# Three edits to a four-batch attention and feed-forward kernel: narrower column tiles for one batch's value products, two weights taken by halves of the tokens, one load placed three steps on

## The chip, the cores and the metric

The kernel runs on one core of a Trainium2 chip. The metric is the device time of one execution in microseconds. Before the change it is 664.37 us, the median of three runs (662.48, 664.87 and 664.37).

## What is computed

Four batches of 768 tokens and eight heads of 64 go through a local attention with block summaries, then through a token-mixing product and a two-layer feed-forward part. Cut to what matters:

```
B, H, S, D = 4, 8, 768, 64                  block, window = 32, 16
k_sum = max over each block of 32 keys      v_sum = mean over each block of 32 values
scores = concat(q k^T / 8 where |i-j| < 16, q k_sum^T / 8 + log 32)
a = softmax(scores)                          x = a @ concat(v, v_sum)      (heads side by side: 768 x 512)
u = x + (x^T U V)^T                          U: 768 x 32, V: 32 x 768
out = u + max(u @ w_ch1, 0) @ w_ch2          w_ch1: 512 x 2048, w_ch2: 2048 x 512
```

## The kernel before

**Staging.** Batch 0's attention runs alone at the start, in an order written out by hand in the string `START`; each word is one step of one head and half (`S` scores, `E` exponentials, `T` transposes, `C` their copies, `V` value products, `N` normalising, `M` block means and so on). Then the feed-forward part of batch 0 runs with the attention of batch 1 between its products, and so on: while TensorE works through batch b's feed-forward part (`up_phase`, 54 steps, then `down_phase`, 96 steps, one for each of 16 weight blocks times 6 tiles of 128 tokens), the attention of batch b+1 is dealt out between these steps.

**Value products of batch 0.** `values(st, h, a)` (L471 to L486) multiplies, for each of three tiles of 128 queries, the exponentials of 64 queries (the stationary operand, 120 rows by 64 columns) with the 120 value rows that this half sees (65 columns wide, the last of ones). The two halves of a tile go to the two halves of the output's partitions, so each instruction uses half of the array's columns. A float32 matmul of the program is two MATMUL records in the trace, so that the 96 matmuls of batch 0 are 192 records at L480. The later batches do the same with `square_values` (L488), by 32 queries and with a tile position for each quarter (L494). `block_means` (L293) also works by 32 columns, alternating between two of the four quarters in one call; `spread_v` (L1016) and `mix_t` (L667) work by 32 columns too.

**The later batches' attention.** `later_step(st, i)` (L544) is step i of 32 for batches 2 and 3. Every third step starts a head. The first 15 steps are spread over the 54 steps of the up phase at places `4 + i * 50 // 15`, so step 2 stands at place 10, step 5 at 20, step 8 at 30, step 7 at 27 and step 10 at 37. The value summaries of heads 4 to 7 need the block sums of the values: `load_vsum(st, 1, i)` (L239) issues two DMAs of 128 x 512 float32 (256 KB each, L253) into buffers of the tag `val`, of which there are eight and which the outputs `o` use too; `add_vsum` (L256) queues the halving adds of these two on GpSimd, one for each step of the phase (`drip`). The sums are first read by step 16, which stands in the down phase, as a copy by ScalarE (L340).

**Queues.** All DMAs are issued by SyncE in program order, those of the weights (`fetch_weight`, L874 to L879, names `whole`) among them. ScalarE casts each fetched weight (L186), takes the exponentials (L413), copies the value summaries (L340) and copies the products of the up phase out of PSUM (L1236, L1248, L1261, L1224), all in program order. TensorE's next product into a bank waits for such a copy.

**The end.** In `down_phase` the six accumulators `acc` stand in six banks; weight block f goes over the six token tiles, three matmuls each (high and low parts). After block 15's three matmuls of a tile, VectorE adds its accumulator to `x` (L1295). Then, for the last batch, `finish` (L1300) runs eight times, for two halves of the tokens and four blocks of 128 columns: three transposes into a bank `ps_o` (L740), a copy by ScalarE (L1303), and a DMA of 192 KB (L1305). `gates` (L1268) prepares the next block's operands `gh` and `gl` on ScalarE and VectorE (L1271, L1272); both have two buffers.

Of the kernel before, what the change touches and what calls it, by code (L numbers as in the profile page):

```python
# [31 lines left out]
DV = D + 1  # L32
NC = DM // P
NF = DF // P
# [52 lines left out]
def body(ctx: ExitStack, tc, q0, q1, k, v, vn, uv, w1, w2, mask, ident, rep, out):  # L87
    nc = tc.nc
# [10 lines left out]
    def bank(name):  # L99
        return psum.tile([P, 512], F32, name=name, tag="bank")  # L100
# [33 lines left out]
    for i in range(4):  # L134
        t = op_place(i)
# [81 lines left out]
    def load_qk(st, h):  # L217
        load_k(st, h)
        load_q(st, h)
# [19 lines left out]
    def load_vsum(st, g, i):  # L239

        parts = 2
        n = BLOCK * D // (2 * parts)
        spare = None
        if st.b == 1 or st.b == 2 and g == 0:
            spare = hidden_place(2 + i)
        st.vn[g, i] = []
        for j in range(parts):
            if spare is not None:
                t = spare[:, j * n : (j + 1) * n]
            else:  # L250
                t = mo.tile([P, DM], F32, name="stage", tag="val", bufs=VALS)[:, :n]
            k = i * parts + j
            nc.sync.dma_start(out=t, in_=vn[st.b, g, :, k * n : (k + 1) * n])  # L253
            st.vn[g, i].append(t)

    def add_vsum(st, g, i):  # L256

        for j, t in enumerate(st.vn.pop((g, i))):
            n = t.shape[1] // 2
            while n > D:  # L260
                nc.gpsimd.tensor_tensor(t[:, :n], t[:, :n], t[:, n : 2 * n], ALU.add)
                yield
                n //= 2
            if i == 0 and j == 0:
                st.vsum[g] = small.tile([P, DV], F32, name="vsum")
                nc.gpsimd.memset(st.vsum[g][:, D:], 1.0)
                nc.gpsimd.tensor_tensor(st.vsum[g][:, :D], t[:, :D], t[:, D : 2 * D], ALU.add)
                yield
            else:
                nc.gpsimd.tensor_tensor(t[:, :D], t[:, :D], t[:, D : 2 * D], ALU.add)  # L270
                yield
                nc.gpsimd.tensor_tensor(st.vsum[g][:, :D], st.vsum[g][:, :D], t[:, :D], ALU.add)
                yield
        if i == 1:
            nc.gpsimd.tensor_scalar_mul(st.vsum[g][:, :D], st.vsum[g][:, :D], 1.0 / BLOCK)
# [193 lines left out]
        copy(at.rearrange("k i q -> k (i q)"), ps[:KC, : 3 * P])  # L469

    def values(st, h, a):  # L471
        at = st.at.pop((h, a))
        if h not in st.psx:
            st.psx[h] = bank("ps_x")
        ps = st.psx[h]
        vt = st.vt[h]
        for i in range(3):
            u = 3 * a + i
            for t in range(2):
                nc.tensor.matmul(  # L480
                    ps[64 * t : 64 * t + 64, u * DV : (u + 1) * DV],
                    at[:, i, 64 * t : 64 * t + 64],
                    vt[u % 2][:, (u // 2) * 2 + (t + u) % 2],
                    start=True,
                    stop=True,
                )  # L486

    def square_values(st, h):  # L488
# [44 lines left out]
    slow = []  # L533
# [10 lines left out]
    def later_step(st, i):  # L544

        h, a = divmod(i, 3)
        if a == 0:  # L550
            if 1 <= h <= H:
                send_squares(st, h - 1)
            if 2 <= h <= H + 1:
                fetch_squares(st, h - 2)
            if h < H:
                scores_by_subtiles(st, h)
                exponentials(st, h, 0)
            if 3 <= h <= H:
                load_v(st, h - 1)
        elif a == 1:  # L560
            if h < H:
                exponentials(st, h, 1)
            if h + 1 < H:
                key_maxima(st, h + 1)
            if 1 <= h <= H:
                for t in range(2):
                    value_summaries(st, h - 1, t, nc.scalar.copy)
        else:
            if h + 2 < H:
                load_qk(st, h + 2)  # L570
            if h == 2:
                st.x = mo.tile([P, NU, DM], F32, name="x")
            if 2 <= h <= H + 1:
                square_values(st, h - 2)
                normalise(st, h - 2)
            if h < H:
                turn_squares(st, h)
        if i in (2, 5):
            load_vsum(st, 1, i // 5)
        if i in (4, 7):  # L580
            slow.append(add_vsum(st, 1, i // 7))
        if i in MIX:
            mix(st, 2 * MIX.index(i))
        if i - 1 in MIX:
            mix_back(st, 2 * MIX.index(i - 1))
# [323 lines left out]
    def use_weight(*key):  # L909
        want, t = prepared[len(used)]  # L910
        assert want == key
        used.append(key)
        return t if key[0] == "down" else [t[:, i] for i in range(t.shape[1])]
# [62 lines left out]
    st = sts[0]  # L976
# [114 lines left out]
    steps = one_bank_steps(nxt)  # L1091
# [70 lines left out]
    for f in range(NF):  # L1162
        for hf in range(2):
            g = first.pop() if first else up_out(up(st, hf, f))
# [103 lines left out]
    def gates(st, f):  # L1268
        h = st.h[f // 2][:, f % 2]
        gh, gl = gate_place("gh"), gate_place("gl")  # L1270
        nc.scalar.activation(gh, h, AF.Relu)  # L1271
        nc.vector.scalar_tensor_tensor(gl, h, 0.0, f32(gh), ALU.max, ALU.subtract)  # L1272
        return gh, gl

    def down_phase(st, g):

        acc = []
        for f in range(NF):
            w = use_weight("down", f)
            ahead = gates(st, f + 1) if f + 1 < NF else None  # L1280
            gh, gl = g
            for t in range(NU):
                if f == 0:
                    acc.append(bank(f"acc{t}"))
                sl = slice(t * P, (t + 1) * P)
                for j, (part_w, gt) in enumerate(((0, gh), (0, gl), (1, gh))):
                    nc.tensor.matmul(  # L1287
                        acc[t],
                        gt[:, sl],
                        w[:, part_w],  # L1290
                        start=(f == 0 and j == 0),
                        stop=(f == NF - 1 and j == 2),
                    )
                if f == NF - 1:
                    nc.vector.tensor_tensor(st.x[:, t], st.x[:, t], acc[t], ALU.add)  # L1295
                yield
            prepare()
            g = ahead

    def finish(st, hf, c):  # L1300
        ps = turn_tokens(st, hf, c)
        o = mo.tile([P, DM], F32, name="o", tag="val", bufs=8)[:, :NH]
        nc.scalar.copy(o, ps)  # L1303
        t0 = st.b * S + hf * NH
        nc.sync.dma_start(out=out[c, :, t0 : t0 + NH], in_=o)  # L1305

    def spread(items, first, last):

        at = {}
        for i, x in enumerate(items):  # L1310
            at.setdefault(first + i * (last - first) // len(items), []).append(x)
        return at

    UP, DOWN = 7 * NF // 2 - 2, NF * NU
# [8 lines left out]
    behind = [(finish_first, hf, c) for hf in range(2) for c in range(NC)]  # L1323
    for b in range(1, B):
        cur, ahead, after = ([*sts, None, None][b + i] for i in range(3))
        todo = later_steps(ahead) if ahead else []
        mine, theirs = todo[:FIRST_STEPS], todo[FIRST_STEPS:]
        steps = spread(mine, 4, UP)
        ends = spread(behind, 2, 2 + 2 * len(behind))
        phase = up_phase(cur)  # L1330
        for i in itertools.count():
            try:
                next(phase)
            except StopIteration as end:
                last = end.value
                break
            do(steps.get(i, ()))
            do(ends.get(i, ()))
            tick()
            drip()  # L1340
            if i == UP - 4:
                g = gates(cur, 0)
        steps = spread(theirs, 0, DOWN - 5)
        for i, x in enumerate(last):
            steps.setdefault(1 + 2 * i, []).insert(0, x)
        for i, _ in enumerate(down_phase(cur, g)):
            do(steps.get(i, ()))
            tick()
            drip()
            if after and i % NU == 0:  # L1350
                do([(later_start, after, j) for j in {10: (-6,), 11: (-5,), 12: (-4,), 13: (-3, -1), 14: (-2,)}.get(i // NU, ())])
        behind = [(finish, cur, hf, c) for hf in range(2) for c in range(NC)]
    do(behind)


# [91 lines left out]
```

## Time and profile before

| | |
|---|---|
| median of three runs | 664.37 us |
| the profiled execution: own time, span | 663.06 us, 661.3 us |
| TensorE busy in the span | 638.6 us (97%), 5232 matmul records |
| VectorE, ScalarE, GpSimd busy | 374.4, 357.5, 361.5 us |
| granted TensorE clock over the span | 0.999 |
| moved by DMA | 115.24 MB by one queue, 57.7% of 16 engines' span |
| read from HBM, written | 91.10 MB, 24.12 MB |

The page of the profile gives each engine's busy time, the span in 40 slices, the DMA queues, the chain of work that ended last, the costliest groups of instructions and the DMA issues. The trace gives the instructions in order of time, merged where they are alike, with the idle time of the engine before them and what ended it in brackets; PE is TensorE, PEld its weight loads, DVE VectorE, ACT ScalarE, POOL GpSimd, SPq the queue of SyncE. A table of windows gives each engine's busy time in stretches of the span.

### The profile page before, as it was taken

Reading aid. Unit: us, or ns where it says so; the run is one execution under the profiler, and the core shown is the slowest. Engines: PE = TensorE matmul, PEld = TensorE weight load, DVE = VectorE, ACT = ScalarE, POOL = GpSimd, SP = SyncE. Lnnn points to the kernel's source line nnn. Section 1 sums busy time; section 2 is a strip of 40 time slices with the busy share of each in tenths; the row PEclk is TensorE's granted clock in tenths of the full one; section 3 lists DMA queues with packets and bytes.
Section 4 is the critical chain, followed back from the end, with each engine's and each line's share of the span. In section 5 each row is a group of like instructions: output and inputs, shape, how many; then the busy total and the mean of one; then the engine's idle time right before and its main releaser. Section 6 shows DMA issues by size and latency. Waiting matters only on the chain.

```text
span 661.3 us, 14015 instructions
## 1 busy us (share of the span) xinstructions
PE 638.6 (97%) x5232; PEld 561.1 (85%) x5232; DVE 374.4 (57%) x1008; ACT 357.5 (54%) x801; POOL 361.5 (55%) x402
## 2 busy tenths in 40 slices
PE   5899999999999998999999999999999999999996
PEld 5789888989888998987887899997787899998885
DVE  5578777658678586576544645566554522232223
ACT  4666666654663547665553467665453465553322
POOL 5423985966586777751355577761344365653310
PEclk9999999999999999999999999999999999999999
DMA  8997497765874169796455069786441055342002
GB/s 215 227 371 229 146 303 237 229 205 183 237 227 158 55 218 314 205 263 195 141 147 161 25 194 339 227 249 193 146 121 57 24 184 168 112 127 65 32 1 95
DMA packets 76420, 116.13 MB, mean 176 GB/s; under 512 B 6976, under 2 KB 52928, under 8 KB 76352
## 3 DMA queue, kind: packets, MB, share of 16 engines
q1 hardware_dynamic: 76352, 115.24, 57.7%
q8 instruction: 41, 0.67, 0.4%
q14 instruction: 27, 0.22, 0.1%
HBM read 91.10 MB, written 24.12 MB: 174 GB/s over the span
## 4 chain that ended last, share of the span: by engine, by line
PE 83%; DMA 5%; DVE 4%; ACT 3%; POOL 2%; issue 1%; SPq 1%; ACTq 0%; POOLq 0%; DVEq 0%
PE acc L1287 30%; PE ps_h L1202 24%; PE acc L943 8%; PE ps_h L921 7%; PE ps_x L494 3%; PE ps_s L354 3%; PE ps_o L740 2%; PE ps_s L377 2%; DMA place<-in_q 1%; DMA qz<-in_q 1%; PE ps_m L667 1%; DMA whole<-up 1%; PE ps_t L463 1%; PE ps_x L480 1%; POOL parts L187 1%
## 5 line engine op out<-in xcount | busy, mean ns | idle before, releaser
L187 POOL TENSOR_TENSOR parts<-whole,parts 128x512 fp32r<-128x512 f32 (+1 forms) x144 | 181.7, 1271 | 154.2 <-ACT parts L186 144.7
L1287 PE MATMUL acc<-parts,gh 128*128 128x512 f32 x576 | 192.3, 399 | 0.0
L1202 PE MATMUL ps_h<-op,parts 128*128 128x384 f32 x1008 | 186.5, 338 | 2.2 <-ACT place L1261 1.8
L1202 PEld LDWEIGHTS ps_h<-op,parts 128*128 128x128 f32 x1008 | 173.8, 188 | 5.1 <-ACT place L1261 2.1
L1287 PEld LDWEIGHTS acc<-parts,gh 128*128 128x128 f32 x576 | 108.1, 188 | 23.7 <-issue 1.7
L1287 PE MATMUL acc<-parts,gl 128*128 128x512 f32 x288 | 112.6, 391 | 0.0
L1272 DVE SCALAR_TENSOR_TENSOR gl<-place,gh 128x768 fp32r<-128x768 f32 x48 | 56.2, 1171 | 97.1 <-ACT gh L1271 97.1
L186 ACT CAST parts<-whole 128x512 fp32r<-128x512 f32 (+1 forms) x144 | 83.6, 584 | 8.2 <-DMA whole<-up 7.1
L921 PE MATMUL ps_h<-place 128*128 128x384 f32 x384 | 74.5, 342 | 0.0
L1271 ACT ACTIVATE gh<-place 128x768 fp32r<-128x768 f32 x48 | 40.6, 846 | 60.0 <-PE acc L1287 59.9
L413 ACT ACTIVATE e<-e,neg 128x120 f32<-128x120 f32 x144 | 46.3, 386 | 48.5 <-DVE neg L403 46.0
L943 PE MATMUL acc<-place,gh 128*128 128x512 f32 x192 | 68.4, 410 | 1.3 <-POOL place L187 1.3
L921 PEld LDWEIGHTS ps_h<-place 128*128 128x128 f32 x384 | 65.8, 188 | 1.0 <-DVE place L722 0.3
L162 POOL TENSOR_SCALAR val<-place 128x512 f32<-128x512 f32 (+1 forms) x30 | 47.0, 1583 | 30.7 <-ACT place L149 14.3
L1287 PEld LDWEIGHTS acc<-parts,gl 128*128 128x128 f32 x288 | 54.2, 188 | 9.9 <-DVE gl L1272 0.3
L187 POOL TENSOR_TENSOR place<-val,place 128x512 fp32r<-128x512 f32 x29 | 39.3, 1377 | 18.6 <-ACT place L186 18.6
L187 POOL TENSOR_TENSOR op<-tmp,op 128x384 fp32r<-128x384 f32 x24 | 25.4, 1069 | 39.2 <-ACT op L186 39.2
L943 PEld LDWEIGHTS acc<-place,gh 128*128 128x128 f32 x192 | 35.6, 188 | 10.5 <-POOL place L187 3.2
L403 DVE CUSTOM_DVE_ANT_0 e<-ps_s,mask_sb 128x120 f32<-128x120 f32 x144 | 32.4, 276 | 12.1 <-PE ps_s L377 7.3
L943 PE MATMUL acc<-place,gl 128*128 128x512 f32 x96 | 37.6, 392 | 0.0
L933 ACT ACTIVATE gh<-ps_h 128x384 fp32r<-128x384 f32 x32 | 15.7, 492 | 36.3 <-PE ps_h L921 36.0
L1262 DVE TENSOR_TENSOR place<-place,ps_h 128x384 f32<-128x384 f32 x24 | 13.3, 554 | 33.6 <-ACT place L1261 33.6
(124 smaller groups left out, 861.2 us busy)
## 6 DMA issues: line engine op xcount, KB each, us to landing
place<-in_w SPq DMA_DIRECT2D x32, 512.0 KB, 5.8
whole<-up SPq DMA_DIRECT2D x24, 512.0 KB, 3.9
whole<-down SPq DMA_DIRECT2D x24, 512.0 KB, 3.7
whole<-up SPq DMA_DIRECT2D x24, 384.0 KB, 3.5
vt<-in_v SPq DMA_DIRECT2D x48, 146.2 KB, 3.9
kt<-in_k SPq DMA_DIRECT2D x24, 288.0 KB, 5.1
out_t<-o SPq DMA_DIRECT2D x32, 192.0 KB, 2.4
there<-squares SPq DMA_DIRECT2D x16, 384.0 KB, 4.3
```

What stands on the lines that cost most here:

```text
L162: nc.gpsimd.tensor_scalar(f32(bits), f32(hi), 0.0, None, ALU.mult)
L186: nc.scalar.copy(hi, val)
L187: engine.tensor_tensor(lo, val, f32(hi), ALU.subtract)
L354: nc.tensor.matmul(ps[:, i * KC : (i + 1) * KC], qt[:, 64 + j * P : 64 + j * P + P], kt[:, k0 : k0 + KC], start=True, stop=True,)
L403: nc.vector.tensor_tensor_reduce(out=e[:, u, :], in0=ps[:, i * KC : (i + 1) * KC], in1=mask_sb[:, m, :], scale=-SCALE, scalar=BIG, op0=ALU ...
L413: nc.scalar.activation(e[:, u, :], e[:, u, :], AF.Exp, bias=st.neg[h][:, u : u + 1], scale=-1.0,)
L921: nc.tensor.matmul(ps[:, :NH], w_split[0, f][:, c % 2, part_w, c // 2], ut[:, c, :], start=(n == 0), stop=(n == 3 * NC - 1),)
L943: nc.tensor.matmul(acc[t], gt[:, sl], w_split[1, f][:, part_w], start=(first and j == 0), stop=(last and j == 2),)
L1202: nc.tensor.matmul(ps, a[:, sa, i], b[:, sb, i], start=(first and n == 0), stop=(n == 5), skip_group_check=not first,)
L1271: nc.scalar.activation(gh, h, AF.Relu)
L1272: nc.vector.scalar_tensor_tensor(gl, h, 0.0, f32(gh), ALU.max, ALU.subtract)
L1287: nc.tensor.matmul(acc[t], gt[:, sl], w[:, part_w], start=(f == 0 and j == 0), stop=(f == NF - 1 and j == 2),)
```

## The change

**Value products of batch 0 by 32 queries.** Each matmul of 64 stationary columns becomes two of 32, with a tile position, in the order of the four quarters; the moving operand and the outputs stay.

**Loads of the value sums three steps on.** For batches 2 and 3, the two `load_vsum` of heads 4 to 7 go from the ends of steps 2 and 5 to those of steps 5 and 8, and their adds from steps 4 and 7 to steps 7 and 10.

**The last two weight blocks by halves of the tokens.** For the last batch, the order of the last twelve steps of the down phase becomes block 14 tiles 0 to 2, block 15 tiles 0 to 2, block 14 tiles 3 to 5, block 15 tiles 3 to 5. The four `finish` of the first half of the tokens go behind steps 91, 92, 93 and 94 of 0 to 95, and only the four of the second half stay behind the phase; of these, the copies of the odd column blocks go to VectorE.

```
     def values(st, h, a):
...
-            for t in range(2):
+            for n in range(4):
                 nc.tensor.matmul(
-                    ps[64 * t : 64 * t + 64, u * DV : (u + 1) * DV],
-                    at[:, i, 64 * t : 64 * t + 64],
-                    vt[u % 2][:, (u // 2) * 2 + (t + u) % 2],
+                    ps[32 * n : 32 * n + 32, u * DV : (u + 1) * DV],
+                    at[:, i, 32 * n : 32 * n + 32],
+                    vt[u % 2][:, (u // 2) * 2 + (n // 2 + u) % 2],
                     start=True,
                     stop=True,
+                    tile_position=(0, 32 * n),
                 )
...
-        if i in (2, 5):
-            load_vsum(st, 1, i // 5)
-        if i in (4, 7):
-            slow.append(add_vsum(st, 1, i // 7))
+        if i in (5, 8):
+            load_vsum(st, 1, i // 8)
+        if i in (7, 10):
+            slow.append(add_vsum(st, 1, i // 10))
...
     def down_phase(st, g):
-        acc = []
-        for f in range(NF):
-            w = use_weight("down", f)
-            ahead = gates(st, f + 1) if f + 1 < NF else None
-            gh, gl = g
-            for t in range(NU):
...
+        order = [(f, t) for f in range(NF) for t in range(NU)]
+        if st.b == B - 1:
+            order[-2 * NU :] = sorted(order[-2 * NU :], key=lambda ft: (ft[1] >= NU // 2, ft))
+        acc, got = [], {}
+        for f, t in order:
+            if f not in got:
+                got[f] = (use_weight("down", f), *g)
+                g = gates(st, f + 1) if f + 1 < NF else None
+            w, gh, gl = got[f]
...
     def finish(st, hf, c):
...
-        nc.scalar.copy(o, ps)
+        (nc.vector.tensor_copy if (st.b, hf) == (B - 1, 1) and c % 2 else nc.scalar.copy)(o, ps)
...
         steps = spread(theirs, 0, DOWN - 5)
+        if b == B - 1:
+            for c in range(NC):
+                steps[DOWN - 5 + c] = [(finish, cur, 0, c)]
...
-        behind = [(finish, cur, hf, c) for hf in range(2) for c in range(NC)]
+        behind = [(finish, cur, hf, c) for hf in range(b == B - 1, 2) for c in range(NC)]
```

The first place is TensorE's order near the end of batch 0's attention; `ps_x` are the value products, `ps_v`, `ps_m` and `ps_r` small products of the mixing part. Before:

```order
L463 MATMUL ps_t<-ident_sb,gh 120x128 x6
L480 MATMUL ps_x<-place 64x65 x18
L1016 MATMUL ps_v<-place,ident_sb 32x192 x8
L480 MATMUL ps_x<-place 64x65 x6
L667 MATMUL ps_m<-x,u_sb 32x128 x6
L1016 MATMUL ps_v<-place,ident_sb 32x192 x8
L667 MATMUL ps_m<-x,u_sb 32x128 x6
L685 MATMUL ps_r<-t_766,rep_sb 128x128
L480 MATMUL ps_x<-place 64x65 x12
L667 MATMUL ps_m<-x,u_sb 32x128 x6
```

and the same place of the changed kernel, where the lines stand one or two further down:

```order
L463 MATMUL ps_t<-ident_sb,gh 120x128 x6
L481 MATMUL ps_x<-place 32x65 x36
L1018 MATMUL ps_v<-place,ident_sb 32x192 x8
L481 MATMUL ps_x<-place 32x65 x12
L669 MATMUL ps_m<-x,u_sb 32x128 x6
L1018 MATMUL ps_v<-place,ident_sb 32x192 x8
L669 MATMUL ps_m<-x,u_sb 32x128 x6
L687 MATMUL ps_r<-t_850,rep_sb 128x128
L481 MATMUL ps_x<-place 32x65 x24
L669 MATMUL ps_m<-x,u_sb 32x128 x6
```

The sequence stays; each group of value products has twice as many, of 32 columns, and stands beside other products of 32 columns.

The second place is SyncE's queue in the up phase of batch 1, while batch 2's attention is dealt out; `stage` are the value sums' loads, `whole` the weights' fetches, `o` the outputs of batch 0. Before:

```order
L208 DMA kt<-in_k 128x3x192
L214 DMA qz_84<-in_q 64x3x128
L215 DMA qz_84<-in_q 64x4x128
L253 DMA stage<-in_vn 128x512 x2
L969 DMA out_t<-o 128x384
L878 DMA whole<-up_109 128x768
L969 DMA out_t<-o 128x384
L438 DMA there<-squares 128x768
L969 DMA out_t<-o 128x384
L878 DMA whole<-up_110 128x1024
L969 DMA out_t<-o 128x384
L878 DMA whole<-up_110 128x768
```

and of the changed kernel, from the output that stood behind the loads:

```order
L971 DMA out_t<-o 128x384
L880 DMA whole<-up_109 128x768
L971 DMA out_t<-o 128x384
L438 DMA there<-squares 128x768
L971 DMA out_t<-o 128x384
L880 DMA whole<-up_110 128x1024
L971 DMA out_t<-o 128x384
L880 DMA whole<-up_110 128x768
L208 DMA kt<-in_k 128x3x192
L214 DMA qz_85<-in_q 64x3x128
L215 DMA qz_85<-in_q 64x4x128
L253 DMA stage<-in_vn 128x512 x2
```

The first two loads move behind three weight fetches, four outputs, one store of squares and the next head's keys and queries, to the place where the second two stood; the second two move to the same place one head later.

The third place is TensorE's order at the very end; `acc` are the accumulators of the six token tiles in order of their numbers, `ps_o` the transposes of `finish`. Before:

```order
L1287 MATMUL acc_7409<-parts,gh 128x512
L1287 MATMUL acc_7409<-parts,gl 128x512
L1287 MATMUL acc_7413<-parts,gh 128x512
L1287 MATMUL acc_7413<-parts,gl 128x512
L1287 MATMUL acc_7413<-parts,gh 128x512
L740 MATMUL ps_o<-ident_sb,x 128x128 x24
```

and of the changed kernel:

```order
L742 MATMUL ps_o<-ident_sb,x 128x128 x3
L1296 MATMUL acc_7505<-parts,gh 128x512
L1296 MATMUL acc_7505<-parts,gl 128x512
L1296 MATMUL acc_7505<-parts,gh 128x512
L742 MATMUL ps_o<-ident_sb,x 128x128 x3
L1296 MATMUL acc_7509<-parts,gh 128x512
L1296 MATMUL acc_7509<-parts,gl 128x512
L1296 MATMUL acc_7509<-parts,gh 128x512
L742 MATMUL ps_o<-ident_sb,x 128x128 x12
```

Half of the transposes move in front of the last matmuls, and the other half stays behind them.

More of the change, by code (lines that the diff above doesn't have):

```diff
@@ L1275, in down_phase @@
     def down_phase(st, g):
-        acc = []
-        for f in range(NF):
-            w = use_weight("down", f)
-            ahead = gates(st, f + 1) if f + 1 < NF else None
-            gh, gl = g
-            for t in range(NU):
[L1283 to L1298, printed above, removed]
+        order = [(f, t) for f in range(NF) for t in range(NU)]
[7 more added lines that the diff above has]
+            w, gh, gl = got[f]
+            if f == 0:
+                acc.append(bank(f"acc{t}"))
+            sl = slice(t * P, (t + 1) * P)
+            for j, (part_w, gt) in enumerate(((0, gh), (0, gl), (1, gh))):
+                nc.tensor.matmul(
+                    acc[t],
+                    gt[:, sl],
+                    w[:, part_w],
+                    start=(f == 0 and j == 0),
+                    stop=(f == NF - 1 and j == 2),
+                )
+            if f == NF - 1:
+                nc.vector.tensor_tensor(st.x[:, t], st.x[:, t], acc[t], ALU.add)
+            yield
+            if t == NU - 1:
+                prepare()
     def finish(st, hf, c):
```

## The prediction

> **What bounds the kernel now.** I read the page first, then the table of windows, to find the stretches in which TensorE (PE) idles, and there the instructions in order of time.
>
> ```profile
> span 661.3 us, 14015 instructions
> PE 638.6 (97%) x5232; PEld 561.1 (85%) x5232; DVE 374.4 (57%) x1008; ACT 357.5 (54%) x801; POOL 361.5 (55%) x402
> ```
>
> PE is busy for 638.6 of 661.3 us, and no other engine for over 57%. PE bounds the kernel, and an edit gains only where it shortens PE's work or one of its waits: 22.7 us in all, most of them at the two ends.
>
> ```profile
> core 0: us, PE busy (x) PEld busy (x) DVE busy (x) ACT busy (x) POOL busy (x), PEclk, DMA share, GB/s
> 240.00:250.00 10.00, 10.00 (x81) 9.48 (x79) 8.75 (x29) 4.25 (x11) 4.46 (x6) 1.00 0.92 291
> 250.00:260.00 10.00, 8.18 (x66) 7.53 (x65) 4.91 (x12) 7.30 (x19) 9.19 (x15) 1.00 1.02 318
> 260.00:270.00 10.00, 10.00 (x120) 9.25 (x119) 6.36 (x23) 6.29 (x15) 7.62 (x11) 1.00 0.71 206
> 390.00:400.00 10.00, 10.00 (x83) 9.49 (x82) 3.98 (x18) 6.46 (x16) 5.30 (x6) 1.00 0.90 279
> ```
>
> The first column after the stretch's length is PE. From 240 to 270, where the loads of batch 2 stand and will stand, it is full but for 1.82 us between 250 and 260. The last row is batch 3's turn of the same loads: PE is full there.
>
> **The moved loads.** Why does PE idle at 250? The instructions in order of time there:
>
> ```profile
> 240.87 1.02 SPq L253 DMA_DIRECT2D stage<-in_vn  x2
> 242.46 0.38 SPq L878 DMA_DIRECT2D whole<-up  x1
> 247.04 0.56 DVE L967 TENSOR_TENSOR o<-ps_o,place 128x384 f32<-128x384 f32 x1 [0.70 <-DMA out_t<-o]
> 248.10 0.28 DVE L403 CUSTOM_DVE_ANT_0 e<-ps_s,mask_sb 128x120 f32<-128x120 f32 x1
> 249.08 0.62 ACT L186 CAST parts<-whole 128x512 fp32r<-128x512 f32 x1 [3.14 <-DMA whole<-up]
> 249.61 0.96 ACT L413 ACTIVATE e<-e,neg 128x120 f32<-128x120 f32 x3
> 250.59 1.04 ACT L340 COPY vt<-vsum 24x390 f32<-24x390 f32 x2
> 251.54 0.46 ACT L1261 COPY place<-ps_h 128x384 f32<-128x384 f32 x1
> 252.06 4.26 PE L1202 MATMUL ps_h<-op,parts 128*128 128x384 f32 x23 [1.82 <-ACT place L1261]
> ```
>
> It is a chain of one queue. ACT's cast at 249.08 waits 3.14 us for a weight fetch that was issued at 242.46. Behind the cast stand, in ACT's order, the exponentials, two copies and the copy L1261, and PE waits 1.82 us for that. The fetch stands behind the two value-sum loads in the DMA queue. They are 2 x 262,144 B; at the 291 GB/s of that window that is 1.80 us, and their issue takes 1.02 us of SP's queue. With the loads gone the fetch should land near 247.2, not 249.0. The cast then ends near 247.9, and the exponentials wait for DVE's L403 instead, whose first is done at 248.10 + 0.28 = 248.4. From there ACT needs 0.96 + 1.04 + 0.46 us, and L1261 ends near 250.85. PE was ready 1.82 us ahead of its row, at 250.24, so its wait shrinks to 0.6 us. Besides, DVE waited 0.70 us for an output buffer of the tag that the loads use; with the loads gone that wait should go, L403 begins at 247.4, and nothing of PE's wait is left. Gain 1.2 to 1.8 us; I take 1.6, since both waits hang on the same two loads. From both sides: nothing, if the fetch does not come sooner, and 1.82.
>
> Who pays where the loads arrive? They stand behind the next head's keys and queries, and the second pair one head later:
>
> ```profile
> 250.90 1.08 SPq L253 DMA_DIRECT2D stage<-in_vn  x2
> ACT parts L186 <- DMA whole<-up: 3.1, 1, 3.1
> 292.74 0.70 PE acc L1287 x3
> ```
>
> The first pair goes to where the second stood (250.90), so that place gets nothing new. The second goes to place 30, one us a place further by 240.87 and 250.90, near 262, where the DMA share is 0.71 and another 1.8 us is free. The middle row is the list of ACT's waits from 225 to 300 us: ACT waits for a fetch once, the 3.1 us above, so later fetches have slack. The adds on POOL move to places 27 and 37 on (some 258 to 276 us), out of the stretch where POOL is busy for 9.19 of 10 us into one of 7.62; their first reader stands in the down phase, which begins at 292.74, some 16 us later. Were that cover gone, each us late would be a us on ACT. Batch 3: PE is full there, gain 0.
>
> **The value products of batch 0.** Rows of the trace, start and length first; the last column but brackets is the number of records:
>
> ```profile
> 32.95 2.95 PE L354 MATMUL ps_s<-place 128*128 128x120 f32 x24 [1.60 <-DMA place<-in_q]
> 35.82 1.97 PE L480 MATMUL ps_x<-place 120*64 120x65 f32 x60
> 37.72 0.54 PE L463 MATMUL ps_t<-ident_sb,gl 128*120 128x128 f32 x3
> 40.84 1.49 PE L480 MATMUL ps_x<-place 120*64 120x65 f32 x36
> 42.26 0.86 PE L1016 MATMUL ps_v<-place,ident_sb 128*32 128x192 f32 x16
> 43.05 0.57 PE L480 MATMUL ps_x<-place 120*64 120x65 f32 x12
> 43.54 0.52 PE L667 MATMUL ps_m<-x,u_sb 128*32 128x128 f32 x10
> 45.61 0.92 PE L480 MATMUL ps_x<-place 120*64 120x65 f32 x24
> 46.46 0.41 PE L667 MATMUL ps_m<-x,u_sb 128*32 128x128 f32 x4
> 28.79 1.58 PE L293 MATMUL ps_n<-place,means_w 96*32 96x65 f32 x48
> 30.30 0.54 PE L463 MATMUL ps_t<-ident_sb,gl 128*120 128x128 f32 x3
> 451.00 0.89 PE L494 MATMUL ps_x<-vt,at 120*32 120x65 f32 x48 [0.26 <-ACT parts L186]
> 451.82 0.50 PE L1287 MATMUL acc<-parts,gh 128*128 128x512 f32 x1
> ```
>
> Up to 32.95 PE waits for queries that a full DMA queue brings, so what it saves before is lost in that wait. Behind it the four groups of L480 take, from their start to the next row's, 1.90 + 1.42 + 0.49 + 0.85 = 4.66 us for 132 records. After the change they are 264 records of 32 columns. The nearest row is L494, the same product of a later batch in the same order of quarters: 48 records in 0.82 us, 17.1 ns each, so 264 take 4.51 us: gain 0.15. The short groups beside 32-column work cost 39, 41 and 35 ns a record where the long one costs 31.7; if that surplus (0.28 + 0.11 + 0.09 us) goes, the gain is 0.6. The other end is L293, also of 32 columns but over two quarters at a time: 48 in 1.51 us, 31.5 ns each, 264 in 8.3 us, a loss of 3.6. I take a gain of 0.3, by L494. I count it in full: the chain of waits runs through these rows, and PE's next products follow directly.
>
> The Trainium skill, "TensorE: Matmul & The Clock Gate", section "Wait — 56ns, not 53.3ns?", puts a floor of about 25 ns between the starts of two matmuls however small they are. By that the estimate for 264 is 6.6 us, a loss of 1.9. The 17.1 ns of L494 are below that floor, so here the row decides. "TensorEngine Tiling (Array Packing)", section "Tiling Modes", says that a change of the tiling mode drains the engine; by it the 32-column neighbours would give the 0.6, and no run here shows it yet.
>
> **The end.** PE's matmuls and transposes are the same in number, only in another order.
>
> ```profile
> 645.54 0.85 ACT L1271 ACTIVATE gh<-place 128x768 fp32r<-128x768 f32 x1 [3.23 <-PE acc L1287]
> 646.42 0.96 DVE L1272 SCALAR_TENSOR_TENSOR gl<-place,gh 128x768 fp32r<-128x768 f32 x1 [3.12 <-ACT gh L1271]
> 650.30 4.09 DVE L1295 TENSOR_TENSOR x<-x,acc 128x512 f32<-128x512 f32 x6 [2.92 <-PE acc L1287]
> 653.50 2.79 PE L740 MATMUL ps_o<-ident_sb,x 128*128 128x128 f32 x24
> 654.04 3.16 ACT L1303 COPY o<-ps_o 128x384 f32<-128x384 f32 x8 [7.65 <-PE ps_o L740]
> 654.54 3.79 SPq L1305 DMA_DIRECT2D out_t<-o  x8
> 655.00:659.00 4.00, 1.29 (x12) 1.05 (x10) 0.00 (x0) 2.20 (x6) 0.00 (x0) 1.00 0.89 330
> ```
>
> Before, the transposes begin at 653.5, the first copy ends at 654.52, and eight issues follow until 658.33, the last begun near 657.9; the DMA share is 0.89. After: half of the transposes (2.79 / 2 = 1.4, less the overlap of the ends 1.3 us) go ahead of the last matmul, which ends near 655.0. VectorE's add of the last tile (4.09 / 6 = 0.68 us), until now behind the first half's transposes, is bare: 655.7. Three transposes (0.5 us with their latency), a copy (0.48) and the first issue stands near 656.7, four issues at 3.79 / 8 = 0.47 us bring the last to 658.1, against 657.9. But four outputs stand in the queue, not eight: at 330 GB/s each takes 0.6 us, so the last lands with less of a backlog. By the issue alone the end is 0.2 to 0.5 us later; by the backlog up to 0.5 earlier. I take a gain of 0.2.
>
> Block 15's first matmul now comes three groups (2.04 us) earlier, near 647.5; its `gh` is ready at 646.39 and its `gl`, which the second matmul reads, at 647.38. The cover is 0.2 us thin, and a stall there would cost some tenths.
>
> **Sum.** -1.6 -0.3 -0.2 = -2.1 us on the profiled execution's own 663.06: 660.96. The median of the runs is 664.37, 1.31 above that execution, and the same edit on it gives 662.3.
>
> **Rivals.**
>
> *The wait stays (0.18).* ACT's next exponentials wait for DVE, whose own list is full (8.75 of 10 us), and another wait takes the place of the fetch, so that PE still waits. For it speaks the 248.10 of L403; against it that the 0.70 us wait goes too. Gain 0.5 from the rest: 663.9.
>
> *All at the upper ends (0.18).* 1.8 + 0.6 + 0.5 = 2.9, 661.5, or below 661.05 if the median falls as the profiled execution did.
>
> *The narrow products run at L293's pitch (0.06).* Then the start costs 3.6 us: 1.8 slower than before with the other gains at 1.8, 666.2, and 668.0 without any. It decides from (4.66 + 1.8) / 264 = 24.5 ns a record on. L494's row speaks against it; for it, that the start is PE's longest stretch of short instructions:
>
> ```profile
> 47.33 0.43 PE L667 MATMUL ps_m<-x,u_sb 128*32 128x128 f32 x8 [0.46 <-issue]
> ```
>
> Here PE idles 0.46 us within one group and waits for nothing that the profile shows. By the floor of about 25 ns (the Trainium skill, "TensorE: Matmul & The Clock Gate", section "Wait — 56ns, not 53.3ns?") the estimate is 1.9 lost against 1.8 gained, 664.5.
>
> *The bare add decides the end (0.06).* The end is 0.7 us later, one add: 663.2.
>
> **How the numbers follow.** The forecast has 0.52. Half a per cent, 3.3 us, is about what a measurement of this kernel can tell from no change: the three runs span 2.4 us. Under 661.05 lie 0.15 of the forecast (the scatter of a median), over half of the upper case and a little of the rest: 0.2. Over 667.7 lies the slow case without the other gains, and what I have not seen: 0.05. So 0.75 for the same. The range, 659.9 to 664.7, holds the forecast, the upper case with the scatter below it, and the wait that stays with the scatter above it, and leaves out the narrow products' slow case.
>
> **What would show it.** In the changed kernel's profile: ACT's cast near 247 without 3 us of wait, and PE's 250 to 260 row at 9.5 or more; no new wait of ACT for a fetch behind 262; the groups at L481 with 17 ns a record and not 25 or 31; SP's last issue some 3.1 us behind the end of the last matmul; no idle time in front of block 15's matmuls. The prediction is wrong if PE still waits for L1261, if the narrow groups take over 5 us behind 33, or if the last output is issued over half a us later against the last matmul than worked out here.

## The result: slower by half a per cent

The changed kernel takes 666.09 us, the median of 20 runs (663.79 to 668.80), the kernel before 662.0 us in 20 runs (660.59 to 664.87). The ratio is 1.0054, with a 95% interval of 1.0041 to 1.0066: about 3.6 us slower, where 2.1 us less was forecast (662.3 us, from a median of 664.37 in the first three runs of before). The profiled execution of the changed kernel took 663.79 us and is the fastest of its 20, so its trace shows a small case of the loss.

The page's first lines for the changed kernel:

```profile
span 662.0 us, 14398 instructions
PE 639.7 (97%) x5424; PEld 562.2 (85%) x5424; DVE 375.1 (57%) x1010; ACT 357.6 (54%) x799; POOL 361.7 (55%) x402
```

There are 192 matmul records more, as the edit says, and 383 instructions more: 384 are these matmuls and their weight loads, and elsewhere there is one less. PE's busy time grows by 1.1 us only.

**The moved loads did what was said.** The windows of the changed kernel, with the columns as before:

```profile
250.00:260.00 10.00, 9.80 (x75) 9.08 (x75) 5.36 (x23) 7.05 (x18) 6.00 (x6) 1.00 0.93 283
260.00:270.00 10.00, 9.98 (x103) 9.35 (x105) 6.55 (x20) 7.06 (x16) 7.29 (x11) 1.00 1.04 291
```

PE is full for 9.80 of the 10 us in which it had 8.18, and the DMA share now peaks one window later, at 1.04, where PE is full. Batch 3's window, 390 to 400, is full as before. The waits between 225 and 300 us, line, total, number and longest:

```profile
ACT parts L186 <- DMA whole<-up: 1.0, 2, 0.5
PE ps_h L1204 <- ACT place L1263: 0.2, 1, 0.2
```

ACT's 3.1 us for a weight fetch are two waits of at most 0.5 us, and PE's 1.82 us for the copy behind it (L1261, here L1263) are 0.2. The same place in order of time:

```profile
246.82 0.55 DVE L969 TENSOR_TENSOR o<-ps_o,place 128x384 f32<-128x384 f32 x1
247.84 1.14 ACT L186 CAST parts<-whole 128x512 fp32r<-128x512 f32 x2
250.17 0.27 DVE L403 CUSTOM_DVE_ANT_0 e<-ps_s,mask_sb 128x120 f32<-128x120 f32 x1
250.49 0.97 ACT L413 ACTIVATE e<-e,neg 128x120 f32<-128x120 f32 x3 [1.50 <-DVE neg L403]
252.96 3.23 PE L1204 MATMUL ps_h<-op,parts 128*128 128x384 f32 x17 [0.20 <-ACT place L1263]
```

The casts no longer wait, VectorE's add no longer waits for an output buffer, and the exponentials wait for VectorE's L403, as the working said.

**The start did not.** TensorE's instructions of the changed kernel in order of time:

```profile
23.37 1.23 PE L481 MATMUL ps_x<-place 120*32 120x65 f32 x72
24.42 1.56 PE L293 MATMUL ps_n<-place,means_w 96*32 96x65 f32 x48
27.04 1.52 PE L293 MATMUL ps_n<-place,means_w 96*32 96x65 f32 x45
30.84 0.30 PE L293 MATMUL ps_n<-place,means_w 120*32 120x65 f32 x3 [2.28 <-issue]
32.17 4.38 PE L354 MATMUL ps_s<-place 128*128 128x120 f32 x24
36.48 1.23 PE L481 MATMUL ps_x<-place 120*32 120x65 f32 x71
37.91 0.93 PE L481 MATMUL ps_x<-place 120*32 120x65 f32 x49 [0.21 <-issue]
38.77 0.54 PE L463 MATMUL ps_t<-ident_sb,gl 128*120 128x128 f32 x3
41.88 0.43 PE L481 MATMUL ps_x<-place 120*32 120x65 f32 x16
44.00 1.02 PE L481 MATMUL ps_x<-place 120*32 120x65 f32 x56 [1.68 <-issue]
44.80 0.86 PE L1018 MATMUL ps_v<-place,ident_sb 128*32 128x192 f32 x16
45.45 0.55 PE L481 MATMUL ps_x<-place 120*32 120x65 f32 x24
48.09 0.49 PE L669 MATMUL ps_m<-x,u_sb 128*32 128x128 f32 x9 [0.82 <-issue]
48.92 0.89 PE L481 MATMUL ps_x<-place 120*32 120x65 f32 x48
49.63 0.61 PE L669 MATMUL ps_m<-x,u_sb 128*32 128x128 f32 x12
```

The pitch is no trouble: 72 records in 1.05 us (23.37 to 24.42) and 48 in 0.71 (48.92 to 49.63) are 14.6 and 14.8 ns each, better than L494's 17.1. But four groups are broken in the middle, for 2.28, 0.21, 1.68 and 0.82 us, 4.99 us in all, and in front of each resumption stands "issue": PE waits for no semaphore there, only for its own instructions. The kernel before has one such break, the 0.46 us at 47.33. The breaks also have a regular distance: from one resumption to the next lie 3 + 3 + 24 + 24 + 71 = 125 matmuls, and 49 + 3 + 48 + 3 + 6 + 16 = 125 (groups of L463, L293 and L481 that are not all shown). Counted from 0 over every record of TensorE, weight loads and its queue among them, the resumptions are records 705, 961, 1217 and 1473, each 256 behind the last; that of before is 1217 too (the expectations below write 1218 and 1474 for the same places). What comes every 256 instructions is a transfer of 16 KB in a queue that the list of DMA queues names, here from 19 to 52 us (packets, MB, share):

```profile
q8 instruction: 6, 0.10, 1.3%
```

Six packets, 0.10 MB. In the trace's packets they run from 27.95 to 29.25, 35.31 to 36.45, 41.64 to 42.71 and 45.52 to 46.62 us, and each break ends 1.3 to 1.6 us behind the end of one of them.

A second loss follows the first break. The scores L354 are the same 24 records before and after, 2.95 us then and 4.38 now. The windows of the changed kernel there (PEclk is the third figure from the end):

```profile
30.00:32.00 2.00, 1.16 (x30) 0.90 (x30) 0.18 (x1) 0.29 (x1) 0.70 (x4) 0.95 1.08 236
32.00:34.00 2.00, 2.00 (x18) 1.83 (x9) 0.15 (x1) 1.38 (x5) 1.02 (x3) 0.50 1.01 311
34.00:36.00 2.00, 2.00 (x15) 2.00 (x14) 1.24 (x12) 1.52 (x5) 1.01 (x2) 0.70 1.06 408
```

The granted clock, 1.00 until 30, falls to 0.50 behind the long break: (0.05 + 0.50 + 0.30) x 2 us = 1.7 us of full clock are lost.

Set against the rows of before, step by step, with the place of each row in both:

| from, to | before | after | difference |
|---|---|---|---|
| start of L354 x24 | 32.95 | 32.17 | -0.78 |
| L354 to the value products | 2.87 | 4.31 | +1.44 (clock) |
| value products to L463 | 1.90 | 2.29 | +0.39 (0.21 break) |
| L463 to the next value products | 3.12 | 3.11 | -0.01 |
| these to `ps_v` | 1.42 | 2.92 | +1.50 (1.68 break) |
| `ps_v` to the last value products | 3.35 | 4.12 | +0.77 (0.82 break) |
| the last value products to the next L669 or L667 | 0.85 | 0.71 | -0.14 |
| these twelve records | 1.23 | 0.54 | -0.69 (the break of before is gone) |

The sum is +2.48 us, and the up phase begins 2.49 us later (55.65 against 53.16). The table sets one execution against one, and it hides the first break. In the execution of before, PE waited 1.60 us at 32.95 for queries that landed at 32.81. In that of the changed kernel the same queries landed at 29.68, while PE stood in its break of 2.28 us. In experiments 1 and 3 below, which have no narrow products, they landed at 30.32 and 30.39, and L354 begins at 30.45 and 30.53, not at 32.17. So the first break is not free.

**The end is even.** Some of the last rows of ACT, DVE, SP and PE in the changed kernel:

```profile
646.20 0.85 ACT L1273 ACTIVATE gh<-place 128x768 fp32r<-128x768 f32 x1 [3.23 <-PE acc L1296]
652.54 6.66 SPq L1315 DMA_DIRECT2D out_t<-o  x8
655.79 0.69 DVE L1304 TENSOR_TENSOR x<-x,acc 128x512 f32<-128x512 f32 x1 [0.34 <-PE acc L1296]
656.53 1.31 PE L742 MATMUL ps_o<-ident_sb,x 128*128 128x128 f32 x10 [0.56 <-DVE x L1304]
```

From the start of the last `gh` to the end of the span are 662.0 - 646.20 = 15.80 us, against 661.3 - 645.54 = 15.76.

### The profile page after: what moved, and what is told of

The parts are those of the page before. It is cut to its first block, busy times and chain, and to the rows that moved or that the text cites. A ratio compares the mean times of both kernels' runs of the same rounds, so it can differ in the third digit from the quotient of the medians.

```text
span 662.0 us, 14398 instructions
## 1 busy us (share of the span) xinstructions
PE 639.7 (97%) x5424; PEld 562.2 (85%) x5424; DVE 375.1 (57%) x1010; ACT 357.6 (54%) x799; POOL 361.7 (55%) x402
## 4 chain that ended last, share of the span: by engine, by line
PE 88%; DVE 3%; ACT 2%; POOL 2%; issue 1%; DMA 1%; SPq 1%; POOLq 0%; DVEq 0%; ACTq 0%
PE acc L1296 30%; PE ps_h L1204 26%; PE acc L945 8%; PE ps_h L923 7%; PE ps_x L496 3%; PE ps_s L354 2%; PE ps_o L742 2%; PE ps_s L377 2%; PE ps_t L463 1%; PE ps_x L481 1%; PE ps_m L669 1%; DMA place<-in_v 1%; PE ps_n L293 1%; PE ps_r L687 1%; POOL place L187 1%
## 5 line engine op out<-in xcount | busy, mean ns | idle before, releaser
L403 DVE CUSTOM_DVE_ANT_0 e<-ps_s,mask_sb 128x120 f32<-128x120 f32 x144 | 32.4, 276 | 12.0 <-PE ps_s L377 7.3
```

Of the source, the lines that this page charges most:

```text
L403: nc.vector.tensor_tensor_reduce(out=e[:, u, :], in0=ps[:, i * KC : (i + 1) * KC], in1=mask_sb[:, m, :], scale=-SCALE, scalar=BIG, op0=ALU ...
```

## The experiments

The theory is that the narrow products cost time by their number of instructions: TensorE's instructions come in blocks of 256 by a DMA, and where a block is used up faster than the next can be fetched through a full DMA queue, TensorE stops, and its clock may fall. The rivals are that another of the three edits costs the time, that the 32-column products are slow in themselves, and that the breaks belong to certain steps of the program.

**1. All but the narrow products.** The changed kernel with `values` as it was:

```
-            for n in range(4):
+            for t in range(2):
...
-                    at[:, i, 32 * n : 32 * n + 32],
+                    at[:, i, 64 * t : 64 * t + 64],
...
-                    tile_position=(0, 32 * n),
```

> The changed kernel with batch 0's value products back at 64 queries; the moved loads and the order of the end stay. Theory A (the loss is in TensorE's supply with instructions: the narrow products double the instructions of a stretch in which the next block of 256 is late): no idle time within a group but the one of 0.46 us that the kernel before has, and 1.5 to 2.2 us less than the kernel before (ratio 0.9967 to 0.9977). Theory B (the loss is in the moved loads or in the end, and the narrow products cost the 2.5 us of the profiled execution at most): still 1 to 2 us slower than before.

Measured: 660.91 us (12 runs), ratio to before 0.9975 [0.9960, 0.9989]. The loss is gone. One break is left, at the place and with the record number (1217) of before:

```profile
46.02 0.43 PE L668 MATMUL ps_m<-x,u_sb 128*32 128x128 f32 x8 [0.73 <-issue]
```

**2. The narrow products alone.** The kernel before with the four-quarter form of `values` (the diff of 1 the other way).

> The kernel before with nothing but the value products of batch 0 by 32 queries. Theory A: 4.5 to 6.5 us slower than before (ratio 1.007 to 1.010), with two to four idle times of 0.2 to 2.5 us within groups of TensorE between 25 and 50 us, each 256 TensorE instructions from the last. Theory B: 0 to 2.5 us slower.

Measured: 667.1 us (6 runs), ratio 1.0071 [1.0054, 1.0089], 4.7 us slower. Two long breaks stand at the same record numbers, 705 and 1217; at 961 TensorE idles for 0.08 us only:

```profile
31.84 0.30 PE L293 MATMUL ps_n<-place,means_w 120*32 120x65 f32 x3 [2.37 <-issue]
45.10 1.02 PE L480 MATMUL ps_x<-place 120*32 120x65 f32 x56 [1.96 <-issue]
```

Here both long breaks are followed by a slow clock; windows of the same kernel:

```profile
32.00:34.00 2.00, 2.00 (x32) 1.48 (x30) 0.00 (x0) 1.14 (x4) 0.03 (x1) 0.60 1.03 251
46.00:48.00 2.00, 2.00 (x57) 1.85 (x48) 0.91 (x3) 1.71 (x3) 0.00 (x0) 0.51 0.60 218
```

So this one edit of three costs as much as the whole change or more: by the intervals 3.6 to 5.9 us, against 2.7 to 4.4.

**3. The moved loads alone.** The kernel before with:

```
-        if i in (2, 5):
-            load_vsum(st, 1, i // 5)
-        if i in (4, 7):
-            slow.append(add_vsum(st, 1, i // 7))
+        if i in (5, 8):
+            load_vsum(st, 1, i // 8)
+        if i in (7, 10):
+            slow.append(add_vsum(st, 1, i // 10))
```

> The kernel before with nothing but the two loads of value sums and their adds three steps on. Theory A and the prediction's step: 1.5 to 2.2 us faster (the 1.82 us wait near 250 us is gone, and batch 3 gains 0.3). Theory B: no change or slower.

Measured: 660.51 us (12 runs), ratio 0.9969 [0.9955, 0.9983], 2.1 us faster; from experiment 1's 660.91 us it can't be told. PE's wait for L1261, 1.8 us before, in the list of waits from 225 to 300 us:

```profile
PE ps_h L1202 <- ACT place L1261: 0.2, 1, 0.2
```

This wait is 1.8, 1.4 and 0.9 us in the profiled executions without the moved loads (before, experiments 4 and 2) and 0.2 us in the three with them (experiments 1 and 3, the changed kernel). At the start of this kernel stand two breaks, though its value products are wide:

```profile
39.65 1.05 PE L480 MATMUL ps_x<-place 120*64 120x65 f32 x28 [0.81 <-issue]
45.91 0.43 PE L667 MATMUL ps_m<-x,u_sb 128*32 128x128 f32 x8 [0.67 <-issue]
```

They are at records 961 and 1217, and no slow clock follows. So breaks of up to 0.8 us come without the narrow products too; those of 1.68 us and more stand only in the traces of kernels with them.

**4. The end alone.** The kernel before with the new `down_phase`, the early `finish` and VectorE's copies.

```
+        if st.b == B - 1:
+            order[-2 * NU :] = sorted(order[-2 * NU :], key=lambda ft: (ft[1] >= NU // 2, ft))
...
-        behind = [(finish, cur, hf, c) for hf in range(2) for c in range(NC)]
+        behind = [(finish, cur, hf, c) for hf in range(b == B - 1, 2) for c in range(NC)]
```

> The kernel before with nothing but the last two weights by halves of the tokens, with the early outputs and the copies on two engines. Theory A: within 0.4 us of before (the profiled execution of the changed kernel needs 15.98 us from block 14's first matmul to the end, the one before 15.94). Theory B: 1 us slower or more.

Measured: 662.48 us (12 runs), ratio 0.9994 [0.9974, 1.0014]: no difference that can be told from none. The three edits alone give -2.1 + 4.7 - 0.4 = +2.2 us against the +3.6 of all together, which agrees within their intervals (some 1 us each).

**5. The blocks shifted.** The changed kernel with 128 instructions more at the start: 32 matmuls of one column into a bank that nobody reads, each two records with a weight load each. They run while TensorE would wait for the first loads.

```
+    zeros = const.tile([P, 32], F32, name="zeros")
+    nc.vector.memset(zeros, 0.0)
+    ps = bank("ps_d")
+    for _ in range(32):
+        nc.tensor.matmul(ps[:32, :1], zeros, zeros[:, :1], start=True, stop=True, tile_position=(0, 0))
```

> The changed kernel with 32 matmuls of one column in front of everything, while TensorE has nothing to do before 8 us: 128 instructions more, no time more. Theory A (blocks of 256 instructions that come late): the idle times within groups stay at the same counts of TensorE instructions (705, 961, 1218, 1474 in the profiles so far), and so stand 128 instructions earlier in the program, not within the block means of the last pair any more; the time stays 3 to 6 us above before. Theory B (something of those places in the program, such as the change between column tiles): the idle times stay at the same places of the program, and their counts grow by 128.

Measured: 669.66 us (6 runs), ratio 1.0096 [1.0061, 1.0132]. TensorE in order of time:

```profile
26.93 1.32 PE L293 MATMUL ps_n<-place,means_w 96*32 96x65 f32 x39
30.41 0.47 PE L293 MATMUL ps_n<-place,means_w 96*32 96x65 f32 x9 [2.16 <-issue]
39.59 0.53 PE L293 MATMUL ps_n<-place,means_w 96*32 96x65 f32 x11
42.91 1.83 PE L293 MATMUL ps_n<-place,means_w 120*32 120x65 f32 x37 [2.79 <-issue]
44.68 0.90 PE L463 MATMUL ps_t<-ident_sb,gl 128*120 128x128 f32 x3
45.37 1.49 PE L463 MATMUL ps_t<-ident_sb,gh 128*120 128x128 f32 x6
49.20 0.65 PE L1023 MATMUL ps_v<-place,ident_sb 128*32 128x192 f32 x9 [0.85 <-issue]
55.37 0.43 PE L669 MATMUL ps_m<-x,u_sb 128*32 128x128 f32 x8 [2.34 <-issue]
```

The breaks have moved to other steps. The second long one stood behind 16 records of a group of L481; now it stands in the group of L293 ahead of it, behind 11 of 48 records: 37 + 3 + 6 + 16 = 62 matmuls earlier, 124 of the 128 instructions that were added. The first moved from the group of L293 at 27.04 into the one before, by 63 matmuls: the 9 left of that group, 9 of L463 and 45. Counted over all records, they still stand at 705, 1217 and 1473, and a new one at 1729. At 961 there is none: that fetch ended at 35.35 and TensorE came there at 37.36. So the breaks belong to the count of instructions and not to a step. The size was missed: 3 to 6 us above before were expected, and it is 6.4 (4.0 to 8.8). In the profiled execution the up phase begins 5.56 us later than in that of the changed kernel (61.21 against 55.65). The breaks make 3.15 us of it (8.14 in all against 4.99): the one at 1217 is longer, 2.79 us against 1.68, and the one at 1729, of 2.34 us, is new. The rest stands ahead of the first break, where PE waited 1.38 and 0.67 us for loads.

**6. More instructions at 64 columns.** The kernel before, with one matmul of two columns into unused columns of the same bank behind each value product (192 records and 384 instructions more, as in the change; nobody reads the results).

```
+                nc.tensor.matmul(
+                    ps[64 * t : 64 * t + 64, 400 + 2 * u : 402 + 2 * u],
+                    at[:, i, 64 * t : 64 * t + 64],
+                    vt[u % 2][:, (u // 2) * 2 + (t + u) % 2, :2],
...
```

> The kernel before, value products by 64 queries, with one matmul of two columns more behind each of them, into columns of the bank that nobody reads: as many more instructions as the narrow products bring (384), and almost no more streaming. Theory A: 3 to 6 us slower than before, with idle times of 1 us and more within groups between 25 and 50 us, 256 instructions apart, as with the narrow products. Theory B (the narrow tiles themselves): at most 1.5 us slower, by some 7 ns for each short record, and no idle time above the 0.5 to 1 us that the kernel before has.

Measured: 670.09 us (4 runs, 666.37 to 673.66), ratio 1.0115 [1.0059, 1.0170]. The added records have a price of their own: four of them stand 0.09 us apart from the next row, so all 192 cost some 4.3 us, an estimate. So the time alone does not decide, but the breaks are there too, without any narrower product:

```profile
21.13 0.24 PE L487 MATMUL ps_x<-place 120*64 120x2 f32 x4
21.22 0.34 PE L480 MATMUL ps_x<-place 120*64 120x65 f32 x4
...
30.88 0.30 PE L293 MATMUL ps_n<-place,means_w 120*32 120x65 f32 x3 [0.91 <-issue]
...
37.96 0.22 PE L487 MATMUL ps_x<-place 120*64 120x2 f32 x1 [0.43 <-issue]
```

They stand at records 705, 961 and 1217 again (the third, of 0.90 us, at 44.18). Breaks of 1 us and more were expected; these are 0.43 to 0.91 us, and the clock does not fall. The profiled run is the fastest of the four; the two slowest have mean clocks of 0.993 and 0.992, and no trace shows their breaks. So more instructions are enough for breaks at these places and 32 columns are not needed; how much of the loss they make here is not shown.

**7. A free DMA queue.** Experiment 2 with seven of the ten weight loads of the start held back, by later places in `START` and a one-column write of VectorE into their buffers, so that the queue is nearly empty behind 40 us.

```
...
+        if late:
+            nc.vector.memset(f32(t)[:, :1], 0.0)
...
```

> The kernel before with the narrow products, and with seven of the ten weight loads of the start held back to the end of batch 0's attention by a write of one column each, so that the DMA engines are less full from some 33 us on; the feed-forward part then waits for its weights, and the whole time is not compared. Theory A with the full DMA engines as what makes a block late: the block that was late near 43 us (2.0 us) comes in time, idle 0.5 us or less there, and the block of instructions that is asked for near 38 us begins to move within 1.5 us, not 3 to 4; the idle time near 29 us, ahead of the weight loads, stays. If the instructions are late for another reason, 1 to 2 us stay near 43 us.

Measured: 676.7 us, one run. The loads that come late cost 9.7 us later on: 3.8 us in a wait for ScalarE's `kt`, and 5.9 in this one, from the list of PE's waits from 50 to 90 us:

```profile
PE acc L946 <- ACT place L186: 5.9, 1, 5.9
```

So the whole time is not compared, but the place in question answers the question. Windows of this kernel:

```profile
28.00:34.00 6.00, 3.06 (x63) 2.50 (x57) 2.40 (x8) 2.20 (x6) 3.46 (x11) 0.97 1.12 215
42.00:50.00 8.00, 8.00 (x273) 6.98 (x271) 7.03 (x23) 5.23 (x15) 1.87 (x3) 1.00 0.01 4
```

With a DMA share of 1.12 TensorE still loses 2.94 us at record 705. With 0.01 it is busy for 8.00 of 8.00 us, through the numbers 1217 and 1473, in the same instructions that were broken for 1.96 us in experiment 2. The fetches show in the bandwidth of 40 to 50 us, in slices of 0.25 us, as three lone peaks:

```profile
GB/s 10 0 0 0 0 0 66 0 0 0 0 0 0 0 0 0 0 0 0 66 0 0 0 0 0 0 0 0 0 0 0 0 0 0 66 0 0 0 0 0
q8 instruction: 3, 0.05, 1.7%
```

From TensorE's first record of a block to the start of the next fetch passed 1.1, 0.3 and 1.3 us here; in the changed kernel, with a share of 1.0 to 1.2, it was 3.9, 4.5 and 3.7 for the fetches of the blocks that came late at 705, 961 and 1217, and 1.5 for that at 1473, with a share of 0.74 from 44 to 46 us. So the fetch stands behind the data, and a block that is used up in 4 us is harmless with a free queue and costs 2 with a full one (experiment 2, at 1217).

## Why the prediction was wrong

- **The moved loads: right.** Forecast 1.6 us of gain, 1.2 to 1.8 by the working; alone they gave 2.1 (1.1 to 3.0 by the interval). In the traces PE's wait shrinks by 0.7 to 1.6 us, since its size before differs by execution, and the chain through the fetch, the cast, the exponentials and the copy is the one that was worked out. *The wait stays* is refuted.
- **The narrow value products: wrong, and this decides the case.** The step that failed is "the nearest row is L494 ... 264 take 4.51 us: gain 0.15", together with "I count it in full". The pitch was even underrated: at 14.7 ns, the mean of the two groups above, 264 take 3.9 us, a gain of 0.8 against 4.66, above the upper end of 0.6. But the four groups behind 33 us took 2.29 + 2.92 + 0.35 + 0.71 = 6.27 us with their breaks, over the 5 us that were named as the sign of failure. The cost of a product was taken to be the time that it is busy. The doubled number of instructions was counted nowhere else, and 384 instructions are one and a half blocks of 256 more that must come through the fullest stretch of the DMA queue.
- **The sign was on the table.** The row at 47.33, "0.46 <-issue", was quoted for the rival of L293's pitch and read as a hint of slow short instructions. It was a block that came too late, and it showed that the start already ran at the limit: in the kernel before, the block from record 961 on was used up between 41.28 and 46.60, and the next fetch had ended only at 46.07.
- **The rival that came nearest in time, 666.2, had the wrong mechanism.** *The narrow products run at L293's pitch* needed 24.5 ns a record, and behind 33 us no group took over 18 between its breaks (49 in 0.86 us at 37.91).
- **"Up to 32.95 PE waits for queries": true of one execution only.** In experiments 1 and 3 and in the changed kernel PE waits for no queries there, so time lost ahead of 33 us was not hidden by that wait. By the start of L354, 32.17 against 30.45 in experiment 1, the first break cost some 1.7 us, an estimate from two executions. Behind it the slow clock cost +1.44 us more in L354, a term that the sum had nothing for.
- **The end: a size.** Forecast -0.2 us, measured +0.04 in the trace and -0.4 in experiment 4 with an interval from -1.7 to +0.9. The bare add came as worked out (PE waits 0.56 us for it), and the last issue begins at 658.8, 3.0 us behind the end of the last matmul of `acc` (655.75), where 3.1 was said. The smaller backlog gave 0.2 us and not 0.5: from the end of the last issue to the end of the span were 2.97 us before (658.33 to 661.3) and 2.80 now (659.20 to 662.0). Block 15's first matmuls did not wait.

The sum by measured terms, -2.1 for the loads, +4.7 for the narrow products and -0.4 for the end, has the right sign and is 1.4 us short of the 3.6, with intervals of about 1 us on each term. The profiled executions of the changed kernel and of experiment 1, which differ in the narrow products alone, agree: the up phase begins 3.80 us later (55.65 against 51.85), of 3.94 us in the whole time (663.79 against 659.85). What stays open is the size in single runs. The 20 runs of the changed kernel have mean granted clocks of 0.992 to 1.000, and the 36 runs of experiments 1, 3 and 4 of 0.997 to 1.000 (with one fall to half clock costing 1.7 of 662 us, 0.26%, the lower ones would be two or three such falls; an estimate). Runs with a clock of 1.000 still took 664.9 to 665.8 us, so the clock is not all of it; the breaks' length or the landing of the loads must vary too, and only the profiled runs show either.

## What to carry to other kernels

Count instructions as well as their time: in a stretch in which TensorE runs many short matmuls while the DMA queue is full, halving the work of each and doubling their number can cost more than it saves. Look there for idle time inside a group that ends with "issue"; one such row, however short, can mean that instructions came late there, and then a stretch with more of them may stop for longer. Split such edits: the moved loads alone are 0.31% faster [0.17, 0.45], and the change that holds them is 0.54% slower.

## What the hardware showed that was not expected

- TensorE's instructions came in fetches of 256, one block ahead of use. With a DMA share of 1.0 to 1.2 a fetch began 2.6 to 4.5 us after TensorE entered the block before, took 1.1 to 1.3 us, and where TensorE waited for it, it went on 1.3 to 1.6 us behind its end (all in the changed kernel). Three blocks that were waited for so took 6.1 to 7.1 us (24.04 to 30.84, 30.84 to 37.91 and 37.91 to 44.00). In the kernel before a block passed in 5.35 us without a break (35.93 to 41.28, share 1.0): the fetch had begun after 2.9. With a share of 0.01 a block passed in 2.8 us (44.71 to 47.47 in experiment 7). Behind 60 us a block of the changed kernel lasts 8.4 us and more, and TensorE stops at no block's start. The Trainium skill, "Runtime: NRT & Kernel Launch", section "Instruction fetch mechanics", states blocks of 16 KiB, 256 instructions, fetched by a DMA queue of the sequencer's own, and calls the cost mostly hidden. The blocks agree with the trace; the hiding does not hold in this stretch, and there the measurement decides.
- An idle time of 2 us could be enough for a slow clock: 0.50 for some 3.4 us, 1.7 us lost. It came behind the breaks of 2.28 us in the changed kernel, of 2.37 and 1.96 in experiment 2, of 2.79 in 5 and of 2.94 in 7, but not behind those of 2.16 and 2.34 in 5. In the traces the falls of one execution lie whole multiples of 3.413 us apart (experiment 2: 32.395 and 46.049, four; experiment 7: 33.647, 64.367 and 81.434, nine and five). Counted in stretches of 3.413 us from such a fall, each of these breaks that it followed put 1.96 us or more of idle time into one stretch, while the 2.16 and 2.34 of experiment 5 were divided, 1.54 and 0.62, 0.65 and 1.69. So in these runs the place of a break decided as well as its length. The Trainium skill, "TensorE: Matmul & The Clock Gate", section "What's actually happening", gives half rate after an idle window of about 3.4 us that runs free of the kernel. The half rate, the length of the slow stretch and a window that runs free agree; the idle time that sufficed here is shorter.
- A product of 32 columns in the order of the four quarters ran at 14.6 to 14.8 ns a record, six tenths of the 24.5 ns at which the forecast would have turned. The floor of about 25 ns (the Trainium skill, "TensorE: Matmul & The Clock Gate", section "Wait — 56ns, not 53.3ns?") does not hold for this order.
